# Linformer attention and SwiGLU block: another order of loads and work ahead of the first gate matmul

## The chip, the cores and the metric

The kernel runs on one core of a Trainium2 chip. The metric is device time in microseconds (us), the median of several executions. The kernel before takes about 573.7 us, so 1% is 5.7 us; 2% is the line above which a change counts as faster or slower here.

## The reference

```python
k_proj = einsum('ks,bhsd->bhkd', E, k)          # E, F: [64, 1024]
v_proj = einsum('ks,bhsd->bhkd', F, v)          # q, k, v: [8, 8, 1024, 64] float32
attn   = softmax(q @ k_proj^T / 8)              # 64 columns per row
x      = (attn @ v_proj), heads put side by side: [8192, 512]
out    = (silu(x @ w_gate) * (x @ w_val)) @ w_out   # d_ff = 1536
```

## The kernel before

Rows are worked in 16 chunks of 512; each chunk needs 12 gate and 12 value products (`f_g`, `f_v`) and the output product. The attention of later batches is hidden between those. The first chunk cannot hide anything: before its first gate matmul, E and k must be in and projected, q turned, scores taken, normalized and turned again, and F and v in and projected. That opening is written out by hand. Below, "turned" means transposed on TensorE; a unit (`u_T`, `u_S`, `u_R`, `u_N`, `u_A`) is the attention scores of four of the eight heads for half of a chunk's rows, so the first chunk has units 0 to 3; a pair is two heads, and PV is the product of the normalized scores with the projected v. All loads that cast to bf16 go through GpSimd, in program order, and GpSimd also does most of the normalizing multiplications (`u_N`), so a load behind a multiplication in the program is issued after it.

```python
load_k(0, 0, 4)                       # first half of k, heads 0-3 (GpSimd, casts to bf16)
for which, src in (("E", E), ("F", F)):
    nc.sync.dma_start(out=raw[:], in_=src)        # E, then F, float32, SyncE
# ... memsets, identities ...
load_k(0, 4, 8); load_q(0, 0, 2); load_v(0, (0, 4, 8))
load_w_gv(0, 1); load_w_gv(1, 2); load_w_gv(2, 4) # gate and value weights, slices of 128 columns
warm(8); turn(0); turn(1); warm(7)    # filler matmuls; E and F turned on TensorE
u_KV(0, "k", (0, 4), at="y")          # project k's first half
# ... warm, KT, second half of k, u_T (turn q), u_S (scores, Exp) ...
u_R(0, 0); u_N(0, 0); u_R(0, 2); u_N(0, 2)        # row sums; multiplication by 1/sum
load_w_gv(4, 6, (0,))
u_KV(0, "v", (0, 4), at="y"); warm(1)
u_A(0, 0, nc.scalar)                  # turn the scores of unit 0
# ... R, N of units 1 and 3 ...
u_A(0, 2, nc.scalar)
u_KV(0, "v", (4, 8), at="y")          # project v's second half
# ... further weights, q, wo, k of the next batch ...
u_PV2(0, 0, 0, 0, nc.scalar); u_PV2(0, 0, 1, 0, nc.vector)
u_A(0, 1, nc.scalar); u_A(0, 3, nc.vector)
f_mm(0, 0, 0, 0)                      # first gate matmuls
# ... and
eng = nc.vector if b == 0 and u in (2, 3) else nc.gpsimd   # in u_N
```

The softmax here doesn't subtract the row's maximum and nothing guards it: scores larger than these inputs give would overflow.

## Time and profile before

| | kernel before |
|---|---|
| median of the first three runs | 574.05 us (572.9 to 574.41) |
| span in the trace | 572.4 us |
| TensorE busy, 28 us to the end | 538.1 of 544 us |
| v's second half landed | 20.01 us |
| first gate matmul | 22.57 us |

The page, the windows and the chain are shown and read in the prediction below. Two readings carry the comparison later. The first is the line of loads: when a piece of k or v lands. A trace notes for each load sixteen completions, one per DMA engine; "landed" is the last of them. The second is the start of the n-th tanh of the feed-forward part on ScalarE, a clock that runs the same in all these kernels once the opening is over. In the timeline: start, duration, engine, line, instruction, and in brackets the idle time before it and what ended that.

```profile
25.51 0.60 ACT L334 ACTIVATE th<-gps 128x512 f32<-128x512 f32 x1 [0.94 <-PE gps L322]
...
34.85 0.60 ACT L334 ACTIVATE th<-gps 128x512 f32<-128x512 f32 x1 [1.13 <-PE gps L322]
37.02 0.60 ACT L334 ACTIVATE th<-gps 128x512 f32<-128x512 f32 x1 [0.28 <-PE qTp L193]
```

### The profile page before, as it was taken

Reading aid. Unit: us, or ns where it says so; the run is one execution under the profiler, and the core shown is the slowest. Engines: PE = TensorE matmul, PEld = TensorE weight load, DVE = VectorE, ACT = ScalarE, POOL = GpSimd, SP = SyncE. Lnnn points to the kernel's source line nnn. Section 1 sums busy time; section 2 is a strip of 40 time slices with the busy share of each in tenths; the row PEclk is TensorE's granted clock in tenths of the full one; section 3 lists DMA queues with packets and bytes.
Section 4 is the critical chain, followed back from the end, with each engine's and each line's share of the span. In section 5 each row is a group of like instructions: output and inputs, shape, how many; then the busy total and the mean of one; then the engine's idle time right before and its main releaser. Section 6 shows DMA issues by size and latency. Waiting matters only on the chain.

```text
span 572.4 us, 7867 instructions
## 1 busy us (share of the span) xinstructions
PE 561.2 (98%) x2910; PEld 268.6 (47%) x2967; DVE 336.8 (59%) x580; ACT 237.0 (41%) x416; POOL 107.9 (19%) x121
## 2 busy tenths in 40 slices
PE   8899999999999999999999999999999999999997
PEld 4654544444444444444444444444444444444444
DVE  2787566666466744766556665567546674554550
ACT  1655444353425434444335434354342543443232
POOL 6734131234002400124001330023200220000000
PEclk9999999999999999999999999999999999999999
DMA  9999993539901698037951399204990124100012
GB/s 160 196 200 206 201 161 74 93 64 196 201 37 41 110 190 157 18 75 129 187 108 38 59 179 195 63 22 88 197 176 37 42 52 74 38 37 25 31 39 92
DMA packets 105927, 61.34 MB, mean 107 GB/s; under 512 B 58016, under 2 KB 97696, under 8 KB 105888
## 3 DMA queue, kind: packets, MB, share of 16 engines
q0 software_dynamic: 42288, 29.89, 36.1%
q1 hardware_dynamic: 63312, 30.68, 25.1%
q8 instruction: 23, 0.38, 0.3%
q10 hardware_dynamic: 288, 0.26, 0.1%
q14 instruction: 16, 0.13, 0.1%
HBM read 60.29 MB, written 16.78 MB: 135 GB/s over the span
## 4 chain that ended last, share of the span: by engine, by line
PE 94%; DMA 2%; POOL 1%; ACT 1%; issue 1%; DVE 0%; POOLq 0%
PE yps L360 29%; PE vps L322 29%; PE gps L322 29%; PE kvp L147 3%; PE sc L227 2%; DMA vb<-in_v_dram 2%; PE pv L285 2%; PE aTp L274 0%; ACT xT L135 0%; PE qTp L193 0%; POOL kb L88 0%; PE kTp L172 0%; POOL qb L107 0%; ACT th L334 0%; PE pv L300 0%
## 5 line engine op out<-in xcount | busy, mean ns | idle before, releaser
L341 DVE SCALAR_TENSOR_TENSOR s<-th,gps 128x512 f32<-128x512 f32 x192 | 130.5, 680 | 138.0 <-ACT th L334 137.8
L322 PE MATMUL gps<-xT,wg 128*128 128x512 bf16 (+1 forms) x755 | 195.7, 377 | 1.2
L322 PE MATMUL vps<-xT,wv 128*128 128x512 bf16 (+1 forms) x761 | 195.9, 377 | 0.8
L360 PE MATMUL yps<-wo,hT 128*128 128x512 bf16 (+2 forms) x761 | 191.5, 376 | 0.8
L334 ACT ACTIVATE th<-gps 128x512 f32<-128x512 f32 x192 | 114.6, 597 | 162.6 <-PE gps L322 155.1
L346 DVE TENSOR_TENSOR hT<-s,vps 128x512 bf16<-128x512 f32 x192 | 132.0, 688 | 22.1 <-PE vps L322 1.5
L360 PEld LDWEIGHTS <-hT 128*128 128x128 bf16 x780 | 76.2, 98 | 89.9
L258 POOL TENSOR_TENSOR AAd<-ee,rr 128x512 bf16<-128x512 f32 x52 | 54.1, 1040 | 319.5 <-issue 168.4
L322 PEld LDWEIGHTS <-wv 128*128 128x128 bf16 x776 | 73.9, 98 | 82.9 <-issue 3.3
L322 PEld LDWEIGHTS <-wg 128*128 128x128 bf16 x776 | 74.0, 98 | 81.3 <-issue 0.6
L370 ACT ACTIVATE ysb<-yps 128x512 f32<-128x512 f32 (+1 forms) x65 | 38.4, 590 | 78.1 <-PE yps L360 74.4
L135 ACT CAST xT<-pv 128x512 bf16<-128x512 f32 x62 | 36.1, 585 | 51.3 <-PE pv L285 50.3
L242 DVE TENSOR_REDUCE zz<-ee 128x8 f32<-128x512 f32 x64 | 43.5, 679 | 17.9 <-ACT ee L231 17.9
L231 ACT ACTIVATE ee<-sc 128x512 f32<-128x512 f32 x64 | 37.9, 595 | 17.4 <-PE sc L227 17.4
L285 PE MATMUL pv<-AT,BDV 128*128 128x512 bf16 x60 | 22.6, 379 | 0.1
L227 PEld LDWEIGHTS <-qTd 128*128 128x128 bf16 x208 | 16.0, 98 | 12.3
L227 PE MATMUL sc<-BD,qTd 128*128 128x128 bf16 x208 | 20.1, 219 | 0.1
L135 DVE CAST BDV<-kvp 64x256 bf16<-64x256 f32 x14 | 6.0, 426 | 22.1 <-ACT ks L157 19.1
L258 POOL TENSOR_TENSOR AA<-ee,rr 128x512 bf16<-128x512 f32 x10 | 10.3, 1038 | 35.2 <-DVE rr L244 33.6
L147 PE MATMUL kvp<-kb,ET 128*64 128x512 bf16 (+1 forms) x72 | 15.5, 357 | 1.3 <-DMA kb<-in_k_dram 1.3
L244 DVE RECIPROCAL rr<-zz 128x8 f32<-128x8 f32 x64 | 13.0, 203 | 6.2
L147 PE MATMUL kvp<-vb,FT 128*64 128x512 bf16 (+1 forms) x72 | 15.5, 358 | 1.0 <-DMA vb<-in_v_dram 1.0
(49 smaller groups left out, 144.8 us busy)
## 6 DMA issues: line engine op xcount, KB each, us to landing
out_dram<-ysb SPq DMA_DIRECT2D x63, 256.0 KB, 2.3
qb<-in_q_dram POOLq DMA_DIRECT2D x15, 512.0 KB, 16.6
kb<-in_k_dram POOLq DMA_DIRECT2D x7, 1024.0 KB, 11.6
vb<-in_v_dram POOLq DMA_DIRECT2D x7, 1024.0 KB, 14.2
wo<-in_moe_w_out_dram POOLq DMA_DIRECT2D x2, 768.0 KB, 14.8
wg<-in_moe_w_gate_dram POOLq DMA_DIRECT2D x5, 256.0 KB, 10.4
wv<-in_moe_w_val_dram POOLq DMA_DIRECT2D x5, 256.0 KB, 10.4
kb<-in_k_dram POOLq DMA_DIRECT2D x2, 512.0 KB, 8.7
```

The costliest lines, as they stand in the source:

```text
L135: (nc.scalar.copy if eng is nc.scalar else eng.tensor_copy)(out=out, in_=in_)
L147: nc.tensor.matmul(out=t[lo : lo + 64, h0:h1].rearrange("p h d -> p (h d)"), lhsT=w[:, j, :], rhs=src[b][:, h0:h1, j, :], start=(j == 0), ...
L227: nc.tensor.matmul(out=ps[:, n, :], lhsT=t[:, n, :], rhs=BD[b % 2][:, 4 * g + n, :], start=True, stop=True)
L231: nc.scalar.activation(out=e[:].rearrange("p h j k -> p (h j k)"), in_=ps[:].rearrange("p a k -> p (a k)"), func=AF.Exp, scale=scale,)
L242: nc.vector.reduce_sum(out=z[:], in_=e[:], axis=AX.X)
L258: eng.tensor_tensor(out=a.rearrange("p j h k -> p h j k"), in0=ee.pop((b, u))[:], in1=rr.pop((b, u))[:].unsqueeze(3).to_broadcast([P, 4, 2 ...
L322: nc.tensor.matmul(out=ps[:, ts], lhsT=(wg, wv)[w][:, kt, f * P : (f + 1) * P], rhs=x[:, kt, ts], start=(kt == 0), stop=(kt == NKT - 1),)
L334: nc.scalar.activation(out=th[:], in_=ps[:], func=AF.Tanh, scale=0.5)
L341: nc.vector.scalar_tensor_tensor(out=s1[:], in0=th[:], scalar=1.0, in1=g[:], op0=ALU.add, op1=ALU.mult)
L346: nc.vector.tensor_tensor(out=hT[c][:, f, :], in0=s1[:], in1=ps[:], op=ALU.mult)
L360: nc.tensor.matmul(out=yy[c][:, cs], lhsT=hT[c][:, f, i * P : (i + 1) * P], rhs=wo[:, f, cs], start=(f == 0), stop=(f == NFT - 1),)
L370: nc.scalar.activation(out=ysb[:, cs], in_=yy[c][:, cs], func=AF.Copy, scale=0.5)
```

## The change

The opening is reordered so that v's projection leaves less work behind it. The first half of k comes as float32 through ScalarE's queue and is cast by VectorE and ScalarE. q's first chunk comes in two parts by rows, one of them ahead of k's second half. F is loaded through ScalarE's queue and turned in two halves around k's second projection. v comes in three pieces, the last of two heads, and some of the work on pairs 0 and 1 is done ahead of it. The multiplication of unit 2 moves from VectorE to GpSimd. The loads of weight slices 2 and 3 move behind three multiplications on GpSimd; the gate half of slices 4 and 5 is issued later too.

```diff
@@ u_N
-        eng = nc.vector if b == 0 and u in (2, 3) else nc.gpsimd
+        eng = nc.vector if (b, u) == (0, 3) else nc.gpsimd
@@ opening (cut: helper signatures, some lines of unchanged order)
-        load_k(0, 0, 4)
+        kb[0] = kv_pool.tile(...)
+        kraw = [aw.tile([P, 2, NJ * D], FP32, ...) for tag in ("qTd", "AAd")]
+        for i in range(2):
+            nc.scalar.dma_start(out=kraw[i][:], in_=k[0, 2 * i : 2 * i + 2]...)
-            nc.sync.dma_start(out=raw[:], in_=src)
+            (nc.sync if which == "E" else nc.scalar).dma_start(out=raw[:], in_=src)
-        load_k(0, 4, 8)
-        load_q(0, 0, 2)
-        load_v(0, (0, 4, 8))
+        load_q(0, 0, (0, 2))
+        load_k(0, 4, 8)
+        load_q(0, 0, (2, 4))
+        load_v(0, (0, 4, 6, 8))
-        warm(8); turn(0); turn(1); warm(7)
+        warm(11); turn(0, "v"); warm(4)
+        # 4 heads of kraw cast into kb[0]: VectorE, half of the last one ScalarE
         u_KV(0, "k", (0, 4), at="y")
+        # unit 0: q turned, half of F turned, scores, sums, multiplication
+        load_w_gv(1, 2, (1,))
         u_KV(0, "k", (4, 8), at="y")
+        # other half of F turned; units 2, 1: q turned, scores, sums, multiplication
+        load_w_gv(2, 4)
+        u_KV(0, "v", (0, 4)); warm(1); u_KV(0, "v", (4, 6))
+        u_PV2(0, 0, 0, 0, act)
+        u_A(0, 2, dve)
+        u_KV(0, "v", (6, 8))
+        u_A(0, 1, act); u_PV2(0, 0, 1, 0, act)
+        u_A(0, 3, dve); u_PV2(0, 0, 0, 1, dve)
+        # further weights, q, wo, k of the next batch
         f_mm(0, 0, 0, 0)
+        u_PV2(0, 0, 1, 1, act)
```

More of the change, by code (lines that the diff above doesn't have):

```diff
@@ L85, in load_k @@
     def load_k(b, h0=0, h1=H):
-        if h0 == 0:
+        if b:
             kb[b] = kv_pool.tile([P, H, NJ, D], BF16, name="kb", tag="kb")
@@ L93, in load_v @@
     def load_v(b, heads=(0, H)):
-        t = kv_pool.tile([P, H, NJ, D], BF16, name="vb", tag="vb")
-        vb[b] = t
+        if heads[0] == 0:
+            vb[b] = kv_pool.tile([P, H, NJ, D], BF16, name="vb", tag="vb")
+        t = vb[b]
         for h0, h1 in zip(heads, heads[1:]):
@@ L100, in load_v, with load_q @@
             )
-    def load_q(b, ch, parts=1):
-        t = q_pool.tile([P, H, 4, D], BF16, name="qb", tag="qb")
-        qb[b, ch] = t
-        n = H // parts
-        for i in range(parts):
-            nc.gpsimd.dma_start(
-                out=t[:, i * n : (i + 1) * n].rearrange("p h j d -> p h (j d)"),
-                in_=q[b, i * n : (i + 1) * n].rearrange("h (p c j) d -> p c h (j d)", c=2, j=4)[:, ch],
-            )
+    def load_q(b, ch, js=(0, 4)):
+        if js[0] == 0:
+            qb[b, ch] = q_pool.tile([P, H, 4, D], BF16, name="qb", tag="qb")
+        js = slice(*js)
+        nc.gpsimd.dma_start(
+            out=qb[b, ch][:, :, js, :].rearrange("p h j d -> p h (j d)"),
+            in_=q[b].rearrange("h (p c j) d -> p c h j d", c=2, j=4)[:, ch, :, js, :].rearrange(
+                "p h j d -> p h (j d)"
+            ),
+        )
     def load_w_gv(c0, c1, which=(0, 1)):
@@ L426 @@
     with tc.manual_schedule():
-        load_k(0, 0, 4)
+        kb[0] = kv_pool.tile([P, H, NJ, D], BF16, name="kb", tag="kb")
+        kraw = [aw.tile([P, 2, NJ * D], FP32, name="kraw", tag=tag) for tag in ("qTd", "AAd")]
+        for i in range(2):
+            nc.scalar.dma_start(
+                out=kraw[i][:],
+                in_=k[0, 2 * i : 2 * i + 2].rearrange("h (p j) d -> p h (j d)", j=NJ),
+            )
         ef = []
@@ L439, with turn @@
             nc.vector.memset(BDV[i][:], 0.0)
-        def turn(which):
-            for half in range(2):
-                ps = bank("v", [P, 4, KP], FP32, "efp")
+        def turn(which, at, halves=(0, 1)):
+            for half in halves:
+                ps = bank(at, [P, 4, KP], FP32, "efp")
                 for i in range(4):
@@ L451, in turn @@
                 js = slice(4 * half, 4 * half + 4)
-                copy((nc.scalar, nc.vector)[which], (ET, FT)[which][:, js, :], ps[:])
+                copy(nc.scalar, (ET, FT)[which][:, js, :], ps[:])
         def warm(n):
@@ L461, in warm @@
                 )
+        dve, act = nc.vector, nc.scalar
+        load_q(0, 0, (0, 2))
         load_k(0, 4, 8)
-        load_q(0, 0, 2)
-        load_v(0, (0, 4, 8))
+        load_q(0, 0, (2, 4))
+        load_v(0, (0, 4, 6, 8))
         load_w_gv(0, 1)
-        load_w_gv(1, 2)
-        load_w_gv(2, 4)
-        warm(8)
-        turn(0)
-        turn(1)
-        warm(7)
+        load_w_gv(1, 2, (0,))
+        warm(11)
+        turn(0, "v")
+        warm(4)
+        for h in range(4):
+            for n in range(2):
+                eng = act if (h, n) == (3, 1) else dve
+                ds = slice(256 * n, 256 * (n + 1)) if h == 3 else slice(0, 512)
+                if n == 0 or h == 3:
+                    copy(eng, kb[0][:, h].rearrange("p j d -> p (j d)")[:, ds], kraw[h // 2][:, h % 2, ds])
@@ L474 @@
         u_KV(0, "k", (0, 4), at="y")
-        warm(2)
+        warm(1)
+        u_T(0, 0, "a", act)
         u_KT(0, at="v", prs=(0, 2))
-        warm(2)
-        u_KV(0, "k", (4, 8), at="y")
-        warm(2)
-        u_KT(0, at="v", prs=(2, 4))
-        u_T(0, 0, "a", nc.scalar)
-        u_T(0, 1, "a", nc.vector)
-        u_T(0, 2, "a", nc.scalar)
+        u_T(0, 2, "a", act)
+        turn(1, "a", (0,))
         u_S(0, 0, "g")
-        u_T(0, 3, "v", nc.vector)
-        u_S(0, 2, "g")
-        u_S(0, 1, "a")
@@ L488 @@
-        u_S(0, 3, "a")
         u_R(0, 0)
         u_N(0, 0)
+        load_w_gv(1, 2, (1,))
+        warm(1)
+        u_KV(0, "k", (4, 8), at="y")
+        turn(1, "a", (1,))
+        u_KT(0, at="v", prs=(2, 4))
+        warm(1)
+        u_T(0, 1, "a", act)
+        u_A(0, 0, dve)
+        u_T(0, 3, "a", dve)
+        u_S(0, 2, "g")
         u_R(0, 2)
         u_N(0, 2)
-        load_w_gv(4, 6, (0,))
+        u_S(0, 1, "g")
+        u_R(0, 1)
+        u_N(0, 1)
+        load_w_gv(2, 4)
+        u_S(0, 3, "v")
@@ L494 @@
+        u_R(0, 3)
+        u_N(0, 3)
         u_KV(0, "v", (0, 4), at="y")
         warm(1)
-        u_A(0, 0, nc.scalar)
-        u_R(0, 1)
-        u_N(0, 1)
-        u_R(0, 3)
-        u_N(0, 3)
-        u_A(0, 2, nc.scalar)
-        u_KV(0, "v", (4, 8), at="y")
-        load_w_gv(4, 6, (1,))
+        u_KV(0, "v", (4, 6), at="y")
+        u_PV2(0, 0, 0, 0, act)
+        u_A(0, 2, dve)
+        u_KV(0, "v", (6, 8), at="y")
+        u_A(0, 1, act)
+        u_PV2(0, 0, 1, 0, act)
+        u_A(0, 3, dve)
@@ L504 @@
+        u_PV2(0, 0, 0, 1, dve)
+        load_w_gv(4, 6)
         load_q(0, 1)
-        load_w_gv(6, 8)
-        load_w_gv(8, 10)
-        load_w_gv(10, 12)
+        for f in (6, 8, 10):
+            load_w_gv(f, f + 2)
         load_wo(0)
@@ L510 @@
         load_k(1)
-        warm(1)
-        u_PV2(0, 0, 0, 0, nc.scalar)
-        u_PV2(0, 0, 1, 0, nc.vector)
-        u_A(0, 1, nc.scalar)
-        u_A(0, 3, nc.vector)
         f_mm(0, 0, 0, 0)
+        u_PV2(0, 0, 1, 1, act)
         f_mm(0, 0, 1, 0)
-        u_PV2(0, 0, 0, 1, nc.scalar)
-        u_PV2(0, 0, 1, 1, nc.vector)
         f_mm(0, 1, 0, 0)
```

## The prediction

> **What bounds the kernel now.** I read the page first, then busy time by window, then the chain that ended last in order of time, then the DMA view of two stretches, then the timeline of the first 30 us. The page's first line and the windows say how much room there is:
>
> ```profile
> span 572.4 us, 7867 instructions
> PE 561.2 (98%) x2910; PEld 268.6 (47%) x2967; DVE 336.8 (59%) x580; ACT 237.0 (41%) x416; POOL 107.9 (19%) x121
> 0.00:22.51 22.51, 17.68 (x124) 10.77 (x127) 10.64 (x28) 8.88 (x19) 14.34 (x25) 1.00 1.17 172
> 22.51:28.00 5.49, 5.34 (x45) 4.09 (x44) 3.13 (x6) 2.31 (x5) 4.82 (x7) 1.00 1.45 196
> 28.00:572.00 544.00, 538.14 (x2746) 253.70 (x2798) 323.06 (x548) 225.78 (x394) 88.71 (x90) 1.00 0.59 104
> ```
>
> In the window rows the second figure is TensorE's busy time. From 28 us on it is busy 538.1 of 544 us at full clock, and the diff touches nothing there: TensorE bounds that part, and it will take the same time, wherever it starts. What the change can move is the start-up: the first gate matmul begins at 22.57 us, and of TensorE's 17.68 us before it, 21 `warm` matmuls (7.3 us in the groups by form) are filler. So the whole stake is some 4% of the run. What sets 22.57 is in the chain, read in order of time:
>
> ```profile
> 5.48 0.70 POOL vb L97
> 6.18 13.83 DMA vb<-in_v_dram
> 20.01 0.04 issue
> 20.05 1.07 PE kvp L147 x8
> 21.13 0.02 issue
> 21.15 0.26 ACT BDV L135
> 21.42 0.27 ACT BDV L135
> 21.69 0.05 issue
> 21.74 0.39 PE pv L300 x2
> 22.13 0.60 PE aTp L274 x8
> 22.73 0.56 PE gps L322 x4
> ```
>
> One piece of 13.83 us is a DMA: the second half of v, issued at 6.18 and landed at 20.01. Behind it come 2.56 us of work that cannot start earlier: project it, copy it, PV, turn the last two score tiles, first gate matmul. The DMA does not take 13.8 us by itself; it stands in a line. The projections on the timeline start as their pieces land:
>
> ```profile
> 9.74 1.03 PE L147 MATMUL kvp<-kb,ET 128*64 128x256 bf16 x8 [1.04 <-DMA kb<-in_k_dram]
> 12.29 1.03 PE L147 MATMUL kvp<-kb,ET 128*64 128x256 bf16 x8 [0.27 <-DMA kb<-in_k_dram]
> 17.50 1.03 PE L147 MATMUL kvp<-vb,FT 128*64 128x256 bf16 x8 [0.61 <-DMA vb<-in_v_dram]
> 20.05 1.06 PE L147 MATMUL kvp<-vb,FT 128*64 128x256 bf16 x8 [0.41 <-DMA vb<-in_v_dram]
> ```
>
> Each later half of k or v comes 2.55 us after what stands before it: 1.05 MB of float32 in 2.55 us is 411 GB/s read. The DMA view of 2 to 9 us and of 9.7 to 20 us, which counts written bytes (half of what is read where it casts to bf16), shows the difference between the two parts:
>
> ```profile
> DMA packets 860, 1.23 MB, mean 175 GB/s; under 512 B 47, under 2 KB 732, under 8 KB 860
> DMA packets 3385, 2.05 MB, mean 199 GB/s; under 512 B 1132, under 2 KB 3385, under 8 KB 3385
> ```
>
> From 9.7 us the line runs at its steady 199 GB/s written. Before that it does not: in 7 us it wrote 1.23 MB, of which 0.52 MB were E and F without cast, so it read 0.52 + 2 x 0.70 = 1.9 MB, 274 GB/s. By 9.7 us only E, F and the first half of k (1.57 MB) were needed and in.
>
> **What the Trainium skill says.** "DMA: Bandwidth & Descriptors", section "Issuing engines are not separate DMA queues": loads issued from ScalarE, SyncE or GpSimd share the same 16 DMA engines, and spreading them saves only issue time. The trace agrees as far as it goes: the pieces come one after the other at 411 GB/s. The same page, "Specifications": transfers under 512 B fall below line rate. Here weight pieces of 256 B packets (window of 19 to 21 us) moved 179 to 185 GB/s against 197 to 207: a loss of about a tenth. "VectorE: DVE Perf Modes", "The perf-mode tier table": a float32 copy inside SBUF runs at twice the plain rate; no row of this trace has one. "TensorE: Matmul & The Clock Gate", "What's actually happening": the array starts at half clock and needs about 3.4 us of work; the first 8 `warm` took 3.59 us, the 7 later ones 1.67 us, which agrees, and idle gaps of up to 1.04 us did not cool it.
>
> **The change part by part.**
>
> 1. First half of k: two float32 loads from ScalarE's queue instead of one casting load from GpSimd's, then 4 heads cast by VectorE (the last one half by ScalarE). Bytes read are the same. What can be won is the start: now E and F run alone from about 2.2 us and GpSimd's first packets follow at about 3.7 us; afterwards 1.05 MB of k flows from about 2.2 us beside E. The cast costs 3.5 VectorE copies of 512 columns, which I estimate at 0.35 us each (by the skill's twofold rate; the same cast out of PSUM took 0.69). VectorE was idle there. I expect the first k projection at about 8.5 us instead of 9.74.
> 2. q's first chunk is split by rows into two quarters with 256 B packets, one ahead of k's second half. Bytes are the same; at a tenth less rate 1.05 MB takes some 0.2 us more. The score chain of units 0 and 2 then starts 2 to 3 us earlier, which alone buys nothing, since v is last in the line.
> 3. F is turned in two halves, moved behind score work: 1.09 us of TensorE out of a stretch that waits anyway. Off the path.
> 4. v in three pieces, the last 2 heads instead of 4, and PV of pairs 0 and 1 ahead of it. Total ahead of v's landing stays E, F, k, one q chunk, v: 0.52 + 2.1 + 1.05 + 2.1 = 5.77 MB. At 411 GB/s that is 14.0 us; from 2.2 us it would end at 16.2; plus the 1.7 us by which the slowest DMA engine's share trailed the first one's landing in this trace, 17.9 against the real 20.0. So 2.1 us are lost in start-up. I give part 1 about 1.2 of these, less the 0.2 of part 2: **the last v piece lands about 1.0 us earlier, at 19.0**.
> 5. The tail behind it. Now: 22.57 - 20.01 = 2.56 us. Afterwards: 8 projections of 128 columns, about 0.6 (8 transposes of that width took 0.60 in the chain); two ScalarE copies of 64x64, about 0.21 each (64x128 took 0.262, 64x256 0.366); then on ScalarE in its order the AT copy of unit 1 and the xT copy, 0.586 each by their rows; some 0.1 of hand-over. 0.6 + 0.42 + 1.17 + 0.1 = 2.3. So **0.25 us shorter**. TensorE also has one PV pair instead of two left after the first gate matmul: **0.2 us**.
>
> Sum: 1.0 + 0.25 + 0.2, about 1.45 us. 574.05 - 1.45 = **572.6 us**, a quarter of a percent.
>
> **The rivals.** (a) *The line of transfers is unmoved*: k's raw load and GpSimd's queue share the engines, F and q's quarter interleave with it, and v still lands at 20. For it: the part from 7 to 8 us, where only 107 GB/s were written, is long after the first issue and I don't know its cause. Against it: 2.2 to 4 us plainly lacks work from GpSimd. Gain then 0.4 us, 573.6. (b) *The full 2.1 us come back*: v lands at 17.9, but the score chain must keep up; q's second quarter would land near 12.9, v three pieces later, and transposes, copies, Exp, sums and three multiplications of 1.04 us on GpSimd take about 5 us. It would just do: about 571.3. (c) *GpSimd becomes the bound*: weights 2 to 4 are now issued behind three such multiplications, at 19 us or later instead of 13.9; if the line runs dry for 0.5 to 1 us, the sixth weight slice, which landed at 32.30 (gate) for a use at 33.75, has 1.45 us of slack to lose. That gives back at most 1 us. (d) *The array cools* in a longer gap: half clock for 3.4 us costs at most 1.7 us. The `warm` calls between the waits are there against it.
>
> **Range and chances.** The low end is rival (b) with a shorter tail, 570.9; the high end is (a) plus the runs' own spread (572.9 to 574.41), 574.2. 2% is 11.5 us, half of the whole start-up: faster 0.01, same 0.98, slower 0.01.
>
> **What would show it.** The first k projection at about 8.5 us; the last v projection at about 19.0 in two-head form; first gate matmul at about 21.3; from there the same 538 us of TensorE work per 544 us. If v's last piece still lands at 20 us, step 1 is wrong; if it lands early and the gate matmul does not follow, step 5 or the score chain is; if TensorE idles on weights between 22 and 40 us, rival (c) took it. The prediction would be wrong if the start moved by more than 3 us, or if anything behind 40 us changed.

## The result, and the profile after

The changed kernel took 573.29 us median (572.67 to 573.53, 4 runs) against 573.73 us (572.9 to 574.41, 4 runs): ratio 0.9991, 95% interval 0.9974 to 1.0009. A ratio is the mean time of one kernel's fast runs over the mean of the other's from the same rounds, so it is not quite the ratio of these medians. Measured once more in five rounds with the experiments it took 573.66 us against 573.28: 0.9998, interval 0.9984 to 1.0012. That is "same": the two ratios stand for gains of 0.5 and 0.1 us, and both intervals hold 1.

The first profile of the changed kernel, page and two window rows (us, then busy time of TensorE, its weight loads, VectorE, ScalarE and GpSimd with counts, clock, DMA share, GB/s):

```profile
span 571.7 us, 7944 instructions
PE 564.2 (99%) x2971; PEld 268.5 (47%) x2971; DVE 336.6 (59%) x581; ACT 238.3 (42%) x421; POOL 109.2 (19%) x122
22.00:28.00 6.00, 5.91 (x42) 3.93 (x41) 3.50 (x6) 2.38 (x4) 5.42 (x8) 1.00 1.32 166
32.00:34.00 2.00, 1.56 (x10) 0.62 (x8) 1.38 (x2) 0.26 (x2) 1.34 (x2) 1.00 1.45 197
```

The same two windows of the kernel before:

```profile
22.00:28.00 6.00, 5.85 (x51) 4.49 (x50) 3.47 (x6) 2.72 (x6) 5.33 (x7) 1.00 1.45 196
32.00:34.00 2.00, 2.00 (x11) 0.88 (x9) 1.62 (x3) 0.60 (x1) 0.98 (x2) 1.00 1.45 196
```

Between 22 and 28 us the transfers now run at 166 GB/s instead of 196, and at 32 to 34 us TensorE, which was full before, stands idle for 0.44 us. (TensorE's busy total is 3 us higher than before, but 61 more matmul records are in this trace; some were missing from the other, so that total says nothing.) The timeline of the changed kernel says where the time came from and where it went. The last piece of v, the first gate matmul, the tanhs that answer to those above, and TensorE at 32 us:

```profile
19.07 0.61 PE L149 MATMUL kvp<-vb,FT 128*64 128x128 bf16 x8
21.24 0.60 PE L324 MATMUL gps<-xT,wg 128*128 128x256 bf16 x4
23.86 0.60 ACT L336 ACTIVATE th<-gps 128x512 f32<-128x512 f32 x1 [1.16 <-PE gps L324]
...
32.74 1.04 PE L324 MATMUL gps<-xT,wg 128*128 128x512 bf16 x4 [0.44 <-DMA wg<-in_moe_w_gate_dram]
33.81 0.60 ACT L336 ACTIVATE th<-gps 128x512 f32<-128x512 f32 x1 [1.74 <-PE gps L324]
36.28 0.60 ACT L336 ACTIVATE th<-gps 128x512 f32<-128x512 f32 x1 [0.28 <-PE gps L324]
```

The first tanh comes 25.51 - 23.86 = 1.65 us earlier than before. The lead is still 1.65 at the sixth. At the seventh it is 34.85 - 33.81 = 1.04, at the eighth 37.02 - 36.28 = 0.74: TensorE waited for the seventh weight slice (slice 6 counting from 0), first for its gate half and then for its value half. **The opening gained 1.65 us against this profile, and a new wait took 0.9 us of it back.** Another 0.14 goes at the twelfth tanh; the lead then stays at 0.61 to the end, and the spans differ by 0.73 us.

The new wait has its origin ten microseconds earlier, on GpSimd. Its timeline in the changed kernel:

```profile
13.59 1.04 POOL L260 TENSOR_TENSOR AA<-ee,rr 128x512 bf16<-128x512 f32 x1 [2.69 <-DVE rr L246]
14.58 0.80 POOL L117 DMA_DIRECT2D wv<-in_moe_w_val_dram  x1
17.28 2.04 POOL L260 TENSOR_TENSOR AA<-ee,rr 128x512 bf16<-128x512 f32 x2 [1.89 <-ACT ee L233]
19.27 0.80 POOL L117 DMA_DIRECT2D wg<-in_moe_w_gate_dram  x1
20.07 0.75 POOL L117 DMA_DIRECT2D wv<-in_moe_w_val_dram  x1
```

The gate weights of slices 2 and 3 are issued at 19.27 us, behind the two multiplications; in the kernel before they were issued at 13.93. GpSimd stood idle for 1.89 us just before those multiplications. The times of slice 6 add up: in the kernel before its gate half landed at 32.30 us and was first used at 33.79. A lead of 1.65 us asks for it at 32.14; it landed at 32.69, and the matmul began at 32.74, 0.60 us late.

### The profile page after: what moved, and what is told of

Read it like the earlier page. It is cut to its first block, busy times and chain, and to the rows that moved or that the text cites. A ratio compares the mean times of both kernels' runs of the same rounds, so it can differ in the third digit from the quotient of the medians.

```text
span 571.7 us, 7944 instructions
## 1 busy us (share of the span) xinstructions
PE 564.2 (99%) x2971; PEld 268.5 (47%) x2971; DVE 336.6 (59%) x581; ACT 238.3 (42%) x421; POOL 109.2 (19%) x122
## 4 chain that ended last, share of the span: by engine, by line
PE 92%; DMA 3%; DVE 2%; POOL 1%; ACT 1%; issue 0%; DVEq 0%; POOLq 0%
PE yps L362 29%; PE vps L324 27%; PE gps L324 27%; PE kvp L149 3%; PE sc L229 2%; PE pv L287 2%; DMA wv<-in_moe_w_val_dram 2%; DMA qb<-in_q_dram 1%; DVE zz L244 1%; POOL AA L260 0%; POOL wg L117 0%; PE qTp L195 0%; DVE hT L348 0%; ACT xT L137 0%; DVE s L343 0%
## 5 line engine op out<-in xcount | busy, mean ns | idle before, releaser
L324 PE MATMUL gps<-xT,wg 128*128 128x512 bf16 (+1 forms) x776 | 197.8, 377 | 0.7 <-DMA wg<-in_moe_w_gate_dram 0.4
L362 PE MATMUL yps<-wo,hT 128*128 128x512 bf16 (+1 forms) x780 | 194.5, 376 | 0.0
L260 POOL TENSOR_TENSOR AA<-ee,rr 128x512 bf16<-128x512 f32 x11 | 11.4, 1038 | 36.3 <-DVE rr L246 34.4
L149 PE MATMUL kvp<-vb,FT 128*64 128x512 bf16 (+2 forms) x80 | 15.7, 339 | 0.3 <-ACT BDV L137 0.3
```

Of the source, the lines that this page charges most:

```text
L149: nc.tensor.matmul(out=t[lo : lo + 64, h0:h1].rearrange("p h d -> p (h d)"), lhsT=w[:, j, :], rhs=src[b][:, h0:h1, j, :], start=(j == 0), ...
L260: eng.tensor_tensor(out=a.rearrange("p j h k -> p h j k"), in0=ee.pop((b, u))[:], in1=rr.pop((b, u))[:].unsqueeze(3).to_broadcast([P, 4, 2 ...
L324: nc.tensor.matmul(out=ps[:, ts], lhsT=(wg, wv)[w][:, kt, f * P : (f + 1) * P], rhs=x[:, kt, ts], start=(kt == 0), stop=(kt == NKT - 1),)
L362: nc.tensor.matmul(out=yy[c][:, cs], lhsT=hT[c][:, f, i * P : (i + 1) * P], rhs=wo[:, f, cs], start=(f == 0), stop=(f == NFT - 1),)
```

## The experiments

Leads are against the first profile of the kernel before, in us, at the sixth and the eighth tanh and at the end of the span; the drop from sixth to eighth is the wait for weights. The medians of the kernel before in the same rounds were 573.27 to 573.74 us.

| run | v in | first gate | lead 6th | lead 8th | lead end | ratio (95%) |
|---|---|---|---|---|---|---|
| before, first profile | 20.01 | 22.57 | 0 | 0 | 0 | 1 |
| before_again | 19.86 | 22.42 | 0.15 | 0.15 | 0.14 | one run |
| changed, first profile | 18.69 | 21.24 | 1.65 | 0.74 | 0.73 | 0.9991 (0.9974 to 1.0009) |
| after_again | 19.44 | 22.78 | 0.11 | -0.47 | -0.49 | 0.9998 (0.9984 to 1.0012) |
| w_early | 18.66 | 21.09 | 1.80 | 1.77 | 1.72 | 0.9981 (0.9969 to 0.9993) |
| k_gpsimd | 18.77 | 21.16 | 1.73 | 0.90 | 0.93 | 1.0002 (0.9986 to 1.0019) |
| kg_w_early | 19.23 | 21.63 | 1.26 | 1.26 | 1.26 | 0.9987 (0.9974 to 1.0000) |
| kg_F_sync | 18.85 | 21.24 | 1.65 | 0.92 | 0.94 | 0.9993 (0.9980 to 1.0006) |
| w_early_v2 | 18.23 | 20.97 | 1.91 | 1.91 | 1.89 | 0.9984 (0.9972 to 0.9996) |
| w_early_v2_warm | 18.81 | 21.55 | 1.34 | 1.34 | 1.31 | 0.9988 (0.9974 to 1.0001) |
| raw_k_only | 18.36 | 25.27 | -2.71 | -2.71 | -2.69 | 1.0060 (1.0042 to 1.0079) |
| before_F_act | 18.51 | 23.20 | -0.64 | -0.64 | -0.63 | 1.0006 (0.9993 to 1.0019) |
| before_q_between | 19.70 | 25.50 | -2.94 | -2.94 | -2.93 | 1.0027 (1.0011 to 1.0043) |
| F_act_warm | 19.10 | 21.66 | 0.90 | 0.90 | 0.91 | 0.9993 (0.9980 to 1.0006) |

A profile is one execution, and the opening differs from one to the next (before_again, after_again), so leads under about 0.5 us between two rows are not read as effects. The wait for weights, in contrast, is either there (0.58 to 0.91 us) or not (0.03 at most).

The leads also flatter. The profiled execution of the kernel before took 574.16 us, near the top of that kernel's range (572.57 to 574.48), so a lead is some 0.5 us more than the gain in the medians: w_early leads by 1.72 us in its trace and by 1.23 in its median. And the profiled executions of after_again (574.67), before_F_act (574.80) and before_q_between (577.11, the other five 574.10 to 574.52) are each the slowest of their runs: their rows show what can happen, not what usually does.

My theory after the result: the late issue of weight slices 2 and 3 took the gain back, and the raw load of k brought v in earlier. The rivals: the line of loads is simply full, so that the order of issue does not matter; and some other part of the change brings v in earlier.

**w_early: the weights of slices 2 and 3 ahead of the multiplications.**

```diff
+        load_w_gv(2, 4)
         u_S(0, 2, "g")
         u_R(0, 2)
         u_N(0, 2)
         u_S(0, 1, "g")
         u_R(0, 1)
         u_N(0, 1)
-        load_w_gv(2, 4)
```

> The changed kernel with one thing moved: the loads of weight slices 2 and 3 are issued on GpSimd before the multiplications of score units 2 and 1, not behind them (its trace has GpSimd idle from 15.4 to 17.3 us, room for both). Theory (weights): the changed kernel gains 1.65 us up to the third gate matmul and gives 0.9 us back in two waits for weight slice 6 (0.61 for the gate half, 0.29 for the value half), because these loads were issued at 19.3 us and the line of transfers ran at 148 to 181 GB/s instead of 196 between 20 and 28 us. Then here slice 6 lands before its use, no TensorE wait on a weight is left, and the lead over the kernel before at the 12th tanh is about 1.5 us instead of 0.61: about 572.4 us timed, ratio to before 0.997. Rival (the line is simply full, and the order of issue does not matter): slice 6 still lands at 32.7 us and the wait stays, ratio 0.999.

Measured: 572.51 us (572.21 to 572.83, 6 runs) against 573.74; no wait of TensorE for a weight is left. GpSimd, and the same window and tanhs as above:

```profile
15.21 0.75 POOL L117 DMA_DIRECT2D wg<-in_moe_w_gate_dram  x1
16.38 0.74 POOL L117 DMA_DIRECT2D wv<-in_moe_w_val_dram  x1 [0.43 <-DMA vb<-in_v_dram]
17.14 2.05 POOL L260 TENSOR_TENSOR AA<-ee,rr 128x512 bf16<-128x512 f32 x2
...
33.05 0.60 ACT L336 ACTIVATE th<-gps 128x512 f32<-128x512 f32 x1 [1.13 <-PE gps L324]
35.25 0.60 ACT L336 ACTIVATE th<-gps 128x512 f32<-128x512 f32 x1 [0.28 <-PE gps L324]
```

```profile
22.00:28.00 6.00, 5.90 (x42) 3.90 (x40) 3.44 (x7) 2.47 (x5) 4.25 (x7) 1.00 1.45 196
```

The multiplications start no later than before (17.14 against 17.28), the line runs at 196 GB/s, and the lead stays: 34.85 - 33.05 = 1.80, 37.02 - 35.25 = 1.77. The theory of the weights holds; of the 1.5 us expected at the twelfth tanh 1.62 came. It holds in all profiles of this opening: in the four that issue these loads late (changed, after_again, k_gpsimd, kg_F_sync) the line ran at 146 to 172 GB/s from 22 to 28 us and slice 6 was waited for; in the four that issue them early it ran at 196 to 197 and nothing waited. Why the line takes until about 29 us to recover, though GpSimd issued a load about every 0.75 us from 19.3 us on, no run shows. The packets in the traces say this much: from 22 to 28 us no packet took over 0.06 us in the four early profiles, while in each of the four late ones 38 to 49 packets took over 0.1 us, the longest 0.53 to 0.73.

**k_gpsimd: the raw load of k undone in the changed kernel.**

```diff
-        kraw = [...]; two nc.scalar.dma_start(...)
+        load_k(0, 0, 4)
-        (the casts of kraw into kb[0])
```

> The changed kernel with the raw load of the first half of k undone: it comes as a casting load from GpSimd, first in its queue, as in the kernel before. Theory (raw k brings v in earlier): the last v piece lands at about 20 us again instead of 18.7, with one DMA engine about 1 us behind the other fifteen from the first load on; the start of gate matmuls is back near 22.3 us, and the time is that of the kernel before within 0.5 us (ratio 0.999 to 1.001). Rival (the order of q, k and v brings it): v still lands at 18.7 to 19.0 and the start stays near 21.2 us.

Measured: v was in at 18.77 us, the first gate matmul at 21.16; timed, 573.26 us (572.97 to 575.64, 6 runs). The raw load is not needed for the earlier v; the rest of the change does as well without it. Whether it can bring v in by itself is the next question. The wait for weights (0.83 us) is the same.

**raw_k_only: the raw load and its casts alone, in the kernel before.**

```diff
-        load_k(0, 0, 4)
+        kb[0] = ...; kraw = [...]; two nc.scalar.dma_start(...)
         warm(8); turn(0); turn(1); warm(7)
+        (the casts of kraw into kb[0])
         u_KV(0, "k", (0, 4), at="y")
```

> The kernel before with only the raw load of the first half of k and its casts on VectorE and ScalarE; everything else as before. Theory (raw k brings v in earlier): v's second half lands at about 18.7 to 19.0 us, the first gate matmul follows 2.5 us later at about 21.4, and since the weights keep their old issue order no wait on slice 6 appears: about 1.1 us faster than before, ratio 0.998. Rival: v's landing does not move (20.0) and nothing is gained.

Measured: 576.94 us, 0.6% slower. v was in at 18.36 us, as theory said: with the raw load alone in the kernel before, v did come in earlier, in this one profile. It did not help. TensorE's timeline shows why:

```profile
6.01 1.07 PE L452 MATMUL efp<-ident_fp,Eraw 64*128 64x64 f32 x8 [1.60 <-DMA Eraw<-in_E_dram]
8.94 1.11 PE L452 MATMUL efp<-ident_fp,Fraw 64*128 64x64 f32 x8 [1.85 <-DMA Fraw<-in_F_dram]
10.12 3.15 PE L464 MATMUL warm<-zeros 128*128 128x512 bf16 x7
13.20 1.51 PE L147 MATMUL kvp<-kb,ET 128*64 128x256 bf16 x8
```

With k's float32 beside them, E and F land later, F at 8.80 instead of 5.66 us. F's turn still stands ahead of k's projection, so TensorE waits for F; its clock falls to half (granted clock 0.50 from 7.3 to 14.2 us), and the seven warm-ups take 3.15 us instead of 1.67. k is projected at 13.20 instead of 9.74, and now the score chain, not v, comes last. So the place of F's turn, which the prediction called off the path, decides whether the raw load costs anything; that moving the turn alone would mend it is argued here, since no run did only that.

**before_again: the kernel before, once more.** No edit.

> The kernel before, unchanged, profiled once more, to see what of its start is the same in each execution. If the one late DMA engine (0.9 to 1.15 us behind the others from the first load of k on) is a property of the kernel, it shows again and v's second half lands at 20.0 us; if it is chance of one execution, v lands anywhere between 19.1 and 20 us.

Measured: v in at 19.86 us, and again one DMA engine had k's first half at 9.56 us when the next slowest had it at 8.27 (9.70 and 8.55 in the first profile).

**before_F_act: only F's queue moved.**

```diff
-            nc.sync.dma_start(out=raw[:], in_=src)
+            (nc.sync if which == "E" else nc.scalar).dma_start(out=raw[:], in_=src)
```

> The kernel before with one edit: F's load is issued on ScalarE's queue beside E's, not behind E on SyncE's. With the raw load of k undone, the changed kernel still had v in at 18.77 us and no late DMA engine, so something else in it took the lag away; what is left is F's queue or the order of the loads. Theory F: the first half of k is in on all 16 engines by 7.9 us as there, v's second half lands at about 19.0, the first gate matmul follows at 21.5, about 1 us faster than before. Theory order: one engine lags again (k's first half in at 9.6), v lands at 19.9 to 20.0, time as before.

Measured: k's first half was in on all engines by 8.16 us and v at 18.51, as the theory of F's queue says. The gate matmuls began later all the same, at 23.20:

```profile
1.20 3.59 PE L458 MATMUL warm<-zeros 128*128 128x512 bf16 x8 [1.20 <-DVE zeros L434]
5.00 1.11 PE L446 MATMUL efp<-ident_fp,Eraw 64*128 64x64 f32 x8 [0.22 <-DMA Eraw<-in_E_dram]
6.26 1.11 PE L446 MATMUL efp<-ident_fp,Fraw 64*128 64x64 f32 x8
7.45 3.15 PE L458 MATMUL warm<-zeros 128*128 128x512 bf16 x7
10.53 1.91 PE L147 MATMUL kvp<-kb,ET 128*64 128x256 bf16 x8
```

TensorE was at half speed until over 12 us, although the eight warm-ups took the same 3.59 us as in the first profile of the kernel before, where the next seven ran at full speed (1.67 us). In before_again, the same kernel, they did not:

```profile
7.10 3.06 PE L458 MATMUL warm<-zeros 128*128 128x512 bf16 x7
```

The traces' clock records begin, at full clock, at 5.25 us in the first profile, at 9.94 in before_again and at 12.81 here (`prof` prints a clock of 1.00 where there is no record yet). So a late full clock also happens without the edit, and this one profile does not show that F's queue caused it. The six timed runs spread from 572.63 to 574.80 us, and this one was the slowest.

**F_act_warm: the same, with three warm-ups moved ahead of the turns.**

```diff
-        warm(8)
+        warm(11)
...
-        warm(7)
+        warm(4)
```

> The kernel before with F's load on ScalarE's queue, and three of the seven warm-up matmuls that stand behind the turns of E and F moved ahead of them (11 and 4 instead of 8 and 7, 15 as before). Theory: moving F's queue alone brought v in at 18.5 us, 1.5 us earlier, and lost it because TensorE had not reached full clock (its 7 later warm-ups took 3.15 us instead of 1.67, the first projection 1.91 instead of 1.03). With the clock up, the first k projection starts at about 8.6 us, v lands at about 18.5, the first gate matmul follows at about 21.1, no weight is waited for since their issue order is that of before, and the lead in the trace is 1.3 to 1.5 us: about 572.3 us, ratio 0.997 to 0.998, as much as the changed kernel with its weights mended, from an edit of two lines. Rival (the raw k load, the split q and the three-piece v are needed for the lead): the lead stays under 0.6 us.

Measured: the clock was up, v in at 19.10 us, the first gate at 21.66, lead 0.90 with no wait for weights; timed, 0.9993 with an interval that holds 1. Between the theory (1.3 to 1.5) and the rival (under 0.6): two small edits of the kernel before give what the whole change gives in these timings, neither told from no gain. That the moved warm-ups brought the clock up is likely but not shown, since it also differs between executions of one kernel.

**before_q_between: q between k's halves, in the kernel before.**

```diff
-        load_k(0, 4, 8)
         load_q(0, 0, 2)
+        load_k(0, 4, 8)
```

> The kernel before with q's load (two DMAs by heads, as before) put between k's two halves. Theory order (k's second half directly behind its first on GpSimd's queue slows one engine): the lag goes away, the first half of k is in by 7.9 us and v's second half lands at about 19.0; since k's second half comes 2.7 us later, the scores move but v stays last: 1 us faster than before or a little less. Theory F: the lag of 0.9 to 1.2 us stays, v lands at 19.9 to 20.0, time as before or slower.

Measured: the lag of one engine stayed (9.41 against 8.45), v was in at 19.70. TensorE waited 2.95 us for k's second half and dropped to half clock in this execution (granted clock 0.64 and 0.50 from 14 to 18 us); the time rose by 0.27%. So order alone does not remove the lag.

**kg_F_sync: the changed kernel with k by GpSimd and F behind E on SyncE.** The edit is that of k_gpsimd, and that of before_F_act undone.

> The changed kernel with the first half of k by GpSimd's casting load, as in an earlier run, and F's load back behind E's on SyncE's queue; all else as changed. Theory F: in that earlier run, with F on ScalarE's queue, all engines had k's first half in by 7.9 us; here one DMA engine lags again by 0.9 to 1.3 us, k's first half is in at 9.4 to 9.7 and the last v piece at 19.7 to 20.0, though the order of q, k and v is the changed one. Rival (F's queue was chance, the order of the loads matters): no lag, v in at 18.7 to 19.2.

Measured: a lag of only 0.39 us (8.26 against 7.87), v in at 18.85. So F's queue is not the cause by itself either. The lag of 0.96 to 1.29 us appeared in the three profiles that had F behind E on SyncE and all of k, and q by heads, through GpSimd, and in no other. In the kernel before, the raw load of k alone (v at 18.36) and F's queue alone (18.51, and 19.10 in F_act_warm) each did without it; what makes it stays open.

**kg_w_early and w_early_v2: is the raw load, or the third piece of v, worth anything once the weights are early?** The edits are k_gpsimd with w_early, and w_early with `load_v(0, (0, 4, 8))` and one `u_KV(0, "v", (4, 8))` in place of two.

> Both edits that did no harm on the changed kernel: the first half of k by GpSimd's casting load again, and the weight slices 2 and 3 issued ahead of the multiplications. If the raw load of k is worth nothing, this equals the run with the weights early alone: lead of 1.6 to 1.8 us over the kernel before in the trace, ratio 0.997 to 0.998. If the raw load is worth something once weights no longer hide it, this is 0.3 us or more behind it.

> The changed kernel with weights early, but v in two pieces of four heads and the second projected whole where the last piece of two heads stood. Theory (the tail): the last piece lands at the same 18.7 us, but its projection is 8 matmuls of 256 columns instead of 128 (about 0.45 us longer) and its two casts on ScalarE are 0.26 us each instead of 0.21, so the first gate matmul is about 0.5 us later than with three pieces and the lead at the 12th tanh falls from 1.6 to about 1.1 us. Rival (the tail is set by the score chain on GpSimd and VectorE, not by the projection): the start moves by less than 0.2 us.

Measured: 572.56 us (0.9987) and 572.28 us (0.9984) against 0.9981 for w_early: three equal results by their intervals. In the traces kg_w_early was 0.46 us behind w_early (1.26 against 1.72), more than the 0.3 that the expectation set as a sign that the raw load is worth something; but its profile was the slowest of its five runs, and the medians are 572.56 and 572.51 us. So the raw load is not shown to be worth anything in the changed kernel, nor to be worth nothing. From v's landing to the first gate matmul it took 2.43 us in w_early, 2.40 in kg_w_early and 2.74 in w_early_v2: the third piece is worth about 0.3 us there. The work behind the start of the last projection was 0.53 us shorter with it (2.17 against 2.70, 0.5 expected), but that projection began 0.26 us after the landing instead of 0.04. And v itself landed 0.43 us earlier in the profile of w_early_v2, and its float32 k, ahead of any difference between the two programs, was in 0.44 us earlier too, so that much is one execution against another.

**after_again: the changed kernel, once more.** No edit.

> The changed kernel, unchanged, for a tighter interval in the same rounds as the run above. By the traces it is 0.6 to 0.75 us ahead of the kernel before: ratio 0.9985 to 0.999. TensorE waits again for weight slice 6, by 0.6 and 0.3 us, if that wait belongs to the kernel and not to one execution.

Measured: the wait for slice 6 is back (0.58 us), but the opening was another:

```profile
1.19 4.20 PE L467 MATMUL warm<-zeros 128*128 128x512 bf16 x11 [1.19 <-DVE zeros L443]
6.63 1.06 PE L455 MATMUL efp<-ident_fp,Eraw 64*128 64x64 f32 x8 [1.23 <-DMA Eraw<-in_E_dram]
7.71 1.63 PE L467 MATMUL warm<-zeros 128*128 128x512 bf16 x4
9.27 1.92 PE L149 MATMUL kvp<-kb,ET 128*64 128x256 bf16 x8
```

E was in at 6.49 us, after 1.23 us of idle TensorE, and the matmuls behind it ran at half speed (granted clock 0.50 from 8.0 to 11.4 us). v landed at 19.44 and the first gate followed only 3.34 us later, since the scores were late. This execution lost the whole opening gain. It is the slowest of the five runs; the other four took 572.77 to 573.80 us.

**w_early_v2_warm: 14 warm-ups instead of 11, on w_early_v2.**

> A version meant to beat both: the changed kernel with the weight slices 2 and 3 issued early, v in two pieces, and 14 warm-up matmuls instead of 11 ahead of E's turn, so that they end at about 5.9 us and leave no gap of 0.85 to 1.23 us before E is in, after which TensorE was once at half clock (the second profile of the changed kernel). Theory: the median stays that of the run without the three extra matmuls (572.3 us), and no execution is slow by the cold start: all runs within 572.0 to 572.9. Rival: the three matmuls delay E's turn, the first k projection starts 0.3 us later, and nothing is gained since v sets the end.

Measured: 572.96 us (572.54 to 573.25), ratio 0.9988. The gap before E's turn shrank to 0.27 us and the clock was up, but v landed at 18.81 instead of 18.23 and the median is no better. Not shown to help; the 11 warm-ups of w_early and w_early_v2 gave no slow run in 11.

**A version that beats both.** w_early beats the kernel before by a fifth of a percent, and so does w_early_v2 (intervals wholly under 1). The changed kernel's own two measurements are 0.9991 and 0.9998. It was not timed in the same rounds as these two, so that they beat it too rests on medians of different rounds (572.51 and 572.28 us against 573.29 and 573.66) and on the wait that is gone.

## Why the prediction was right, and where its parts were not

The time, 573.29 us, lies inside the range of 570.9 to 574.2, and "within 2%" was right for the reason given: only the opening, 4% of the run, was at stake. That the number fell inside says little by itself: the range also holds the kernel before's own median, and the forecast gain of 1.45 us was measured as 0.5 and 0.1 us, neither told from none. By its own steps:

1. **First k projection at about 8.5 us**: 8.38 in the first profile. **The raw load of k as the source of the earlier v**: not as told. The prediction gave part 1 "about 1.2 of these" 2.1 us lost in start-up; without the raw load v was in at 18.77 all the same, and in the kernel before F's queue alone (18.51) did as much as the raw load alone (18.36). So the raw load is one of two edits that each came with an earlier v, in single profiles, and they do not add up. A cast of 512 columns lasts 0.49 us on average in the trace, but where casts follow each other (raw_k_only) they start every 0.33 to 0.34 us, as the estimate of 0.35 has it.
2. **v at 19.0 us**: 18.69 in one execution, 19.44 in the other. The size of the term was fair; the cause named was not needed for it, so it came right partly by luck.
3. **F's turn off the path**: right in the changed kernel, but it reads as if the place did not matter. With the turn left in its old place beside the raw load, the opening lost 2.7 us (raw_k_only).
4. **The tail 0.25 us shorter**: not in the first profile. From landing to gate it was 21.24 - 18.69 = 2.55 us against 2.56. The work behind the landing did get shorter: from the start of the last projection to the gate it took 2.17 us in this profile and the same 2.17 in w_early, k_gpsimd, kg_w_early, kg_F_sync and after_again, against 2.52 before, and it ran along ScalarE's row as the estimate had it. What the estimate left out is that TensorE had the transposes of unit 2's scores ahead of that projection, in the order of the program, when v landed: the projection began 0.38 us after the landing, against 0.04 before. In w_early, k_gpsimd, kg_w_early and kg_F_sync that delay was 0.22 to 0.26 us, and landing to gate took 2.39 to 2.43:

```profile
18.72 0.39 PE L276 MATMUL aTp<-ident_bf,AA 128*128 128x128 bf16 x4
19.07 0.61 PE L149 MATMUL kvp<-vb,FT 128*64 128x128 bf16 x8
19.71 0.43 ACT L137 CAST BDV<-kvp 64x64 bf16<-64x64 f32 x2
20.17 0.59 ACT L137 COPY AT<-aTp 128x512 bf16<-128x512 bf16 x1
20.69 0.58 ACT L137 CAST xT<-pv 128x512 bf16<-128x512 f32 x1
```

5. **One PV pair less behind the first gate, 0.2 us**: the gate moved by 1.33 us and the first tanh by 1.65, so 0.32.
6. **The sum of 1.45 us**: the opening gained 1.65 in the first profile. The step that failed is that the sum stopped there. Rival (c) named the very wait (slice 6, 1.45 us of slack, 1.49 with the first use at 33.79 us, weights issued "at 19 us or later instead of 13.9", "at most 1 us" given back) and stood outside the sum. The runs show it in each of the four profiles of this opening with late weights: 0.58 to 0.91 us. With 0.9 us of it taken off, the sum would have been about 0.55 us, and 573.5 us.
7. **Rival (d), the array cools**: also real, in one of two profiles of the changed kernel; the extra 0.9 us there for eight projection matmuls (1.92 against 1.03) are within its "at most 1.7". The prediction held that idle gaps of up to 1.04 us did not cool the array, which is so in its trace; here one of 1.23 us did.

Where the Trainium skill was used: "TensorE: Matmul & The Clock Gate", section "What's actually happening", calls the activity window free-running, and says that the same kernel ramps up differently from run to run. That fits the two profiles of the kernel before, whose first eight warm-ups took the same 3.59 us and whose next seven took 1.67 us in one and 3.06 in the other, though no run here isolates it. "DMA: Bandwidth & Descriptors", section "Issuing engines are not separate DMA queues", says that spreading loads over issuing engines saves only issue time; the runs neither show nor refute it. The raw load of k and F's load, each moved alone to ScalarE's queue in the kernel before, came with a v that was in 1.65 and 1.5 us earlier than in the first profile (0.9 for F in F_act_warm), but in the changed kernel neither was needed for that (18.77 without the raw load, 18.85 without both).

## What to carry to other kernels

When a change lets a stage start earlier, subtract the gain from the slack of everything that the stage will use next, and look at what the same change did to the issue of those loads: here 1.65 us of lead met 1.45 us of slack and loads issued 5 us later. A load that stands behind arithmetic on the engine that issues it is issued when that arithmetic is done (19.27 us here, behind 2.04 us of multiplications), so put it into the idle time ahead of it. And in an opening that lives on warm-up matmuls, a shift of a load can let TensorE fall to half clock, which cost more here than the load was worth (raw_k_only), and one profile cannot tell that from an execution that came out slow by itself.

## What the Trainium skill lacked or had wrong

- "TensorE: Matmul & The Clock Gate", "What's actually happening": names an idle window of about 3.4 us as what brings half clock back, and gives no figure for a window that is idle in part. Here the granted clock fell to 0.50 after a stretch of 3.41 us in which TensorE was busy for 2.16 us (after_again, 4.58 to 7.99 us), with no idle gap over 1.23 us, and it stayed at 1.00 after one with 2.30 us (the kernel before, 8.67 to 12.08).
- "DMA: Bandwidth & Descriptors", "Latency and other measured facts": notes that some DMA engines are usually slower than others. Here one engine of sixteen fell 0.96 to 1.29 us behind the next slowest within the first load of k and carried the lag on to v, in three profiles, and by 0.39 us or less in others; the page gives no size, and no run settled the cause.
- No page was found that tells how fast a GpSimd queue of loads runs when its loads are issued only shortly before their turn: with slices 2 and 3 issued at 19.3 us instead of about 15.2, the transfers ran at 146 to 172 GB/s from 22 to 28 us, against 196 to 197.
